# One transfer for x of batch 1, ahead of the clearing of the padded state tile

## The chip, the cores and the metric

The kernel runs on one core of a Trainium2 chip. Its time is the device time of one execution in microseconds (us); shorter is better. The core has TensorE (PE, with its weight loads listed as PEld), VectorE (DVE), ScalarE (ACT), GpSimd (POOL) and SyncE (SP). Each takes its own instructions in order and waits for the others by semaphores. SP, ACT and GpSimd also issue DMA transfers, each into a queue of its own: in the profile q1 is SP's, q10 ScalarE's and q0 GpSimd's. All three queues are served by the same 16 DMA engines.

## The reference

```python
# x (8, 8, 512, 64), state (8, 8, 32, 64): batches, heads, rows, width
scores = scale * x @ state^T;  a  = softmax(scores);   xread = a @ state
scores2 = scale * state @ x^T; a2 = softmax(scores2);  sread = a2 @ x
attn = concat([xread, sread], rows)            # 512 + 32 rows a batch
x = attn.transpose(0, 2, 1, 3).reshape(4352, 512)
out = (1 / (1 + exp(-(x @ w_gate))) * (x @ w_val)) @ w_out   # 512 -> 1536 -> 512
```

Each batch is a small attention of its rows against 32 state rows for each of eight heads, and of the state rows against the batch's rows; all 4352 rows then pass through one gated layer. Results are float32.

## The kernel before

The whole program is unrolled, and every engine's instructions stand in the order in which the function calls them: a hand-written sequence of small helpers, most with the batch as first argument. Batches 0 and 1 are worked on together in the opening, batches 2 to 7 and the state rows (as a ninth round) follow in a regular loop of twelve steps each. The gated layer never multiplies the attention output by the weights directly: `sw_visit` and its relatives multiply the state by the gate and value weights (tile `SW`), and `gv_mm` multiplies these by the transposed attention weights `aT`, so that the output of the two comes from one product.

The opening does this for batch 0:

- `load_xp(0, nc.sync, lo, n)` (L87) loads x of batch 0 in four transfers of two heads each on SP, in the order heads 0-1, 4-5, 2-3, 6-7. `load_s(0, nc.scalar)` (L524) loads the state of batches 0 and 1 on ScalarE's queue.
- `cast_xp` (L95) casts each quarter to bf16: heads 0-1 and 6-7 on ScalarE, 4-5 and 2-3 on VectorE. `xT_mm` (L132) transposes it on TensorE with the identity `ident`, and `xT_cp` (L135) copies the result out.
- `Sq_mm` (L174) gives the scores of two heads, `Sq_exp` (L182, ScalarE) their exponentials, `nq_sum` (L186 and L188, VectorE) the sums and reciprocals, `nq_mul` (L193, VectorE or GpSimd) the product. On ScalarE all four `Sq_exp` of batch 0 are called behind the cast of heads 6-7.
- `aT_mm` (L234) transposes the attention weights, `aT_cp` (L244) copies them out, and `gv_mm` (L343) and `sw_visit` (L293) can run.

x of batch 1 does not come through SP. `load_xh` (L100) loads it on GpSimd's queue, which turns float32 into bf16 on the way, into the tile `xh` (named `xf` in the profile). `xT_mm(1, 0, ...)` transposes heads 0-3 of it, `xT_mm(1, 2, ...)` heads 4-7. On TensorE the order there is: transposes of heads 6-7 of batch 0, `xT_mm(1, 0)`, the last scores of batch 0, three warm-up matmuls, `xT_mm(1, 2)`.

GpSimd's queue also carries the weights, in the order in which they are needed: `load_w` (L104) eight times with 256 columns and twice with 512, and `load_sb` (L527) with the state of later batches, then x of batch 2 and the output weights. Behind them lie the first casts and products that GpSimd computes itself.

`zero(sbz, pool)` (L111) clears the tile `sbz`, a part of `tw`, in which the state of batches 2 to 7 stands between zeros; `load_sb` writes into it later. `make_identity` writes `ident`. `warm` (L517) issues matmuls on a cleared tile; the first eight stand at the start of TensorE's order.

Of the kernel before, what the change touches and what calls it, by code (L numbers as in the profile page):

```python
# [16 lines left out]
def kernel(  # L17
# [45 lines left out]
    sbz = tw[:, :27 * D].rearrange("p (q d) -> p q d", q=3)  # L63
# [11 lines left out]
    vec, act, pool = nc.vector.tensor_copy, nc.scalar.copy, nc.gpsimd.tensor_copy  # L75
# [13 lines left out]
    def xh_tile(b):  # L89
        if b not in xhs:  # L90
            xhs[b] = stg.tile((128, H, 4, D), BF, name="xf", padded_shape=(128, 2 * H, 4, D))

    def cast_xp(b, cp, lo, n):
        xh_tile(b)
        cp(xhs[b][:, lo:lo + n], xfs[b][:, lo:lo + n])  # L95

    def load_xh(b, lo, n):
        xh_tile(b)
        v = x[b].rearrange("h (p c) d -> p h c d", c=4)
        nc.gpsimd.dma_start(xhs[b][:, lo:lo + n], v[:, lo:lo + n])  # L100
# [9 lines left out]
    def zero(t, eng):  # L110
        (nc.gpsimd if eng is pool else nc.vector).memset(t, 0.0)  # L111
# [401 lines left out]
    def warm(n, place):  # L513

        ps = place[0].tile((128, 512), FP, name="warm", tag=place[1])
        for _ in range(n):
            nc.tensor.matmul(ps.rearrange("p (r k) -> p r k", r=4), wm, wm.unsqueeze(1).to_broadcast((128, 4, 128)), start=True, stop=True)  # L517
# [46 lines left out]
    load_s(0, nc.scalar)  # L564
    nc.vector.memset(wm, 0.0)
    warm(4, S1)
    zero(sbz, pool)
    warm(4, S1)
    make_identity(nc, ident)
    load_xh(1, 0, 4)  # L570
    nc.vector.memset(ones, 1.0)
    cast_s(0, vec)
    cast_xp(0, act, 0, 2)
    load_xh(1, 4, 4)
    zero(sTd, vec)
    sT_mm(0, S1)
    load_xp(0, nc.sync, 4, 2)
# [459 lines left out]
```

## Time and profile before

| | |
|---|---|
| median of 3 runs | 213.55 us |
| lowest, highest | 213.36, 213.91 us |
| span of the profiled execution, first to last instruction | 212.3 us |
| what lies around the span, by the median | 1.25 us |
| TensorE busy in the span | 204.3 us (96%) |
| VectorE, ScalarE, GpSimd busy | 160.3, 129.6, 78.1 us |
| DMA | 27.14 MB, 128 GB/s over the span |

The profile records one execution; of its own time it gives the span alone. Times in its rows are counted from the span's start. A row of the timeline gives start, length, engine, line, operation, the output and the input tile, and in brackets how long the engine had stood idle and what ended that. The chain of waits follows the work that ended last back to what released it at each step. The view of the DMA queues counts packets in a window of time; 1024 packets of 1 KB are x of batch 0.

### The profile page before, as it was taken

The numbers are of one execution on the slowest core, as the hardware profiler recorded it, in microseconds if no ns is written. First come the engines' busy times: TensorE is split into PE (matmuls) and PEld (weight loads), VectorE is DVE, ScalarE is ACT, GpSimd is POOL, SyncE is SP. The second block draws the span as 40 slices with busy tenths as digits, with TensorE's granted clock in tenths as the row PEclk, the third lists the DMA queues.
The fourth block names the chain that finished last, engine by engine and source line by source line (L and its number), as shares of the span: only waits on it lengthen the run. The fifth ranks groups of instructions, "written<-read, shape, count | busy, mean of one in ns | idle before, by whom it ended". The sixth has DMA issues, their size and how long they took to land.

```text
span 212.3 us, 5333 instructions
## 1 busy us (share of the span) xinstructions
PE 204.3 (96%) x2089; PEld 132.9 (63%) x2089; DVE 160.3 (76%) x308; ACT 129.6 (61%) x244; POOL 78.1 (37%) x103
## 2 busy tenths in 40 slices
PE   7779999999999999999999999999999999999991
PEld 2545443677666666575666566657566666788981
DVE  2598899998987788578866887688748876865681
ACT  3878898754767477856786578647764663333210
POOL 8799458599042705900491029201500000000000
PEclk9999999999999999999999999999999999999998
DMA  6999999662589943996822621273110400221133
GB/s 205 163 192 191 214 289 183 119 212 40 78 224 333 136 91 110 302 94 208 249 42 48 173 99 28 58 120 153 29 31 35 166 2 0 99 102 49 39 112 99
DMA packets 41320, 27.14 MB, mean 128 GB/s; under 512 B 23632, under 2 KB 39248, under 8 KB 41296
## 3 DMA queue, kind: packets, MB, share of 16 engines
q1 hardware_dynamic: 31088, 20.00, 36.9%
q0 software_dynamic: 9776, 6.49, 19.8%
q10 hardware_dynamic: 432, 0.33, 0.6%
q8 instruction: 16, 0.26, 0.5%
q14 instruction: 8, 0.07, 0.1%
HBM read 18.35 MB, written 8.91 MB: 128 GB/s over the span
## 4 chain that ended last, share of the span: by engine, by line
PE 91%; DMA 3%; DVE 2%; ACT 1%; SPq 1%; issue 0%
PE gvp L355 30%; PE outp L425 29%; PE gvp L343 10%; PE gvp L358 5%; PE outp L442 4%; PE swp L286 4%; DMA xf<-in_x_dram 3%; PE swp L293 2%; PE outp L484 2%; PE Sp L147 1%; PE outp L467 1%; PE rdp L262 1%; SPq L87 1%; DVE rsq L186 1%; PE aTp L234 1%; PE rdp L265 1%
## 5 line engine op out<-in xcount | busy, mean ns | idle before, releaser
L369 DVE SCALAR_TENSOR_TENSOR glu<-th,gvp 128x512 bf16<-128x512 f32 (+1 forms) x108 | 70.1, 655 | 36.7 <-PE gvp L355 13.7
L364 ACT ACTIVATE th<-gvp 128x512 f32<-128x512 f32 (+1 forms) x108 | 62.1, 578 | 49.3 <-PE gvp L355 34.8
L355 PE MATMUL gvp<-aT,SW 128*128 128x512 bf16 x288 | 77.4, 379 | 0.1
L329 ACT CAST SW<-swp 128x512 bf16<-128x512 f32 x83 | 46.5, 592 | 9.3 <-PE swp L286 8.3
L425 PEld LDWEIGHTS <-Sm 128*128 128x128 bf16 x324 | 31.7, 98 | 12.6
L355 PEld LDWEIGHTS <-SW 128*128 128x128 bf16 x288 | 26.7, 98 | 17.3 <-issue 3.6
L200 POOL CAST Eb<-E 128x256 bf16<-128x256 f32 x32 | 12.8, 438 | 52.0 <-ACT E L167 52.0
L425 PE MATMUL outp<-tw,Sm 128*128 128x256 bf16 x240 | 31.8, 273 | 0.0
L425 PEld LDWEIGHTS <-glu 128*128 128x128 bf16 x240 | 23.5, 98 | 10.2
L425 PE MATMUL outp<-wo,glu 128*128 128x256 bf16 x168 | 22.9, 273 | 0.0
L343 PE MATMUL gvp<-aT,SW 128*128 128x512 bf16 x96 | 22.6, 379 | 0.0
L227 POOL TENSOR_TENSOR ab<-E,ri 128x512 bf16<-128x512 f32 x13 | 14.3, 1100 | 11.8 <-DVE ri L210 7.1
L407 DVE TENSOR_TENSOR Sm<-glu 128x768 bf16<-128x768 bf16 (+1 forms) x34 | 18.0, 535 | 0.0
L433 DVE SCALAR_TENSOR_TENSOR res<-outp,U 128x512 f32<-128x512 f32 x22 | 15.0, 685 | 1.2 <-PE outp L442 0.9
L343 PEld LDWEIGHTS <-SW 128*128 128x128 bf16 x96 | 8.6, 97 | 10.4 <-issue 1.8
L116 POOL CAST xb<-xf 128x1024 bf16<-128x1024 f32 x12 | 13.2, 1128 | 1.9 <-DMA xf<-in_x_dram 1.9
L358 PE MATMUL gvp<-xb,wgv 128*128 128x256 bf16 x96 | 12.6, 272 | 0.0
L167 ACT ACTIVATE E<-Sp 128x512 f32<-128x512 f32 x14 | 8.4, 599 | 6.7 <-PE Sp L147 5.7
L425 PE MATMUL outp<-wo,Sm 128*128 128x256 bf16 x84 | 11.5, 273 | 0.0
L358 PEld LDWEIGHTS <-wgv 128*128 128x128 bf16 x96 | 9.3, 98 | 1.3
L251 POOL CAST xs<-xf 128x1024 bf16<-128x1024 f32 x10 | 10.2, 1044 | 0.0
L425 PE MATMUL outp<-tw,glu 128*128 128x256 bf16 x72 | 9.8, 273 | 0.0
(105 smaller groups left out, 213.3 us busy)
## 6 DMA issues: line engine op xcount, KB each, us to landing
out_dram<-res SPq DMA_DIRECT2D x14, 512.0 KB, 3.4
xf<-in_x_dram SPq DMA_DIRECT2D x5, 1024.0 KB, 7.5
wo<-in_moe_w_out_dram POOLq DMA_DIRECT2D x3, 512.0 KB, 7.8
xf<-in_x_dram SPq DMA_DIRECT2D x4, 256.0 KB, 3.9
wgv<-in_moe_w_gate_dram POOLq DMA_DIRECT2D x4, 256.0 KB, 7.7
wgv<-in_moe_w_val_dram POOLq DMA_DIRECT2D x4, 256.0 KB, 8.8
xf<-in_x_dram POOLq DMA_DIRECT2D x1, 1024.0 KB, 9.5
out_dram<-res SPq DMA_DIRECT2D x3, 256.0 KB, 2.2
```

The costliest lines, as they stand in the source:

```text
L116: cp(xbs[b].rearrange("p c h d -> p h c d")[:, lo:lo + n], (xhs if b in xhs else xfs)[b][:, lo:lo + n])
L200: nc.gpsimd.tensor_copy(Ebs[b][:, c], E1s[b][:, c])
L227: (nc.gpsimd if eng is pool else nc.vector).tensor_tensor(half(b, i, abs_), e1, ri.unsqueeze(len(ri.shape)).to_broadcast(e1.shape), ALU.mult)
L329: cp(*sw_left.pop((b, lo, w, e)))
L343: nc.tensor.matmul(ps, SWs[b][:, g, w, fs], aTs[b][:, :, g], start=(g == 0), stop=(g == 1))
L355: nc.tensor.matmul(ps, SWs[b][:, g, w, fs], aTs[b][:, :, g], start=(g == 0), stop=(g == 1))
L358: nc.tensor.matmul(ps, (wg, wv)[w][:, j, fs], held["XS"][:, j], start=(j == 0), stop=(j == 3))
L364: nc.scalar.activation(th, held["gv", b, f][0], AF.Tanh, scale=0.5)
L369: nc.vector.scalar_tensor_tensor(glus[b][:, f], held["th", b, f], 1.0, held["gv", b, f][1], ALU.add, ALU.mult)
L407: eng.tensor_tensor(S_(b, t)[:, i], a, c, op)
L425: nc.tensor.matmul(wps[key][:, c], lhs[:, i, c * 128:(c + 1) * 128], rhs[:, i], start=(first and c == 0 and i == 0), stop=(i == NF // 2 - ...
L433: nc.vector.scalar_tensor_tensor(to, wps[key], 0.5, held["w", name], ALU.mult, ALU.add)
```

## The change

GpSimd's first work is put in another order, and x of batch 1 is loaded by one transfer of eight heads instead of two of four.

```diff
     load_s(0, nc.scalar)
     nc.vector.memset(wm, 0.0)
     warm(4, S1)
-    zero(sbz, pool)
     warm(4, S1)
     make_identity(nc, ident)
-    load_xh(1, 0, 4)
+    load_xh(1, 0, 8)
+    zero(sbz, pool)
     nc.vector.memset(ones, 1.0)
     cast_s(0, vec)
     cast_xp(0, act, 0, 2)
-    load_xh(1, 4, 4)
     zero(sTd, vec)
     sT_mm(0, S1)
```

On GpSimd, the opening of its order after the program's own constants; `tw` is the tile cleared, `xf` here x of batch 1 and `wgv` the gate and value weights:

```order
-L111 MEMSET tw 128x1728
 masks.py:197 MEMSET ident 128x128
 masks.py:199 ISA
 masks.py:199 AFFINE_SELECT ident<-ident 128x128
-L100 DMA xf<-in_x_dram 128x4x256 x2
+L100 DMA xf<-in_x_dram 128x8x256
+L111 MEMSET tw 128x1728
 L104 DMA wgv<-in_moe_w_gate_dram 128x4x256
 L104 DMA wgv<-in_moe_w_val_dram 128x4x256
```

The clearing moves from the head of the queue to behind the one transfer of x, and ahead of all weights; the identity and the transfer move up by one place.

On TensorE, the second group of transposes of x of batch 1 (`xT_mm(1, 2)`), behind the three warm-up matmuls; `DMASW1` is the semaphore of GpSimd's second transfer:

```order
 L517 LDWEIGHTS wm
 L517 MATMUL warm<-wm 128x512
-L132 LDWEIGHTS xf [waits DMASW1_49]
+L132 LDWEIGHTS xf
 L132 MATMUL xTp<-ident,xf 128x128 [waits PE_49]
 L132 LDWEIGHTS xf
```

The wait for the second transfer is gone there. The first group (`xT_mm(1, 0)`) waits for GpSimd's first transfer as before, which is now the whole of x of batch 1. The order of the instructions on TensorE, VectorE, ScalarE and SP is unchanged.

## The prediction

> **What bounds the kernel now.** I read the page first, then the busy time by stretch, then the chain of waits over the opening, then the order of the opening on GpSimd, then the packets of the DMA queues in short windows.
>
> From the page and from the view of busy time by stretch (stretch, its length, then each engine's busy us):
>
> ```profile
> span 212.3 us, 5333 instructions
> ...
> 14.00:207.00 193.00, 192.87 (x1977) 126.50 (x1977) 151.71 (x284) 120.88 (x229) 65.81 (x81) 1.00 0.55 124
> ```
>
> From 14 us to 207 us TensorE is busy 192.87 of 193 us. So nothing that starts earlier or later behind 14 us is worth much; what counts is when TensorE reaches that dense stretch. The chain of waits (start, length, what) tells what sets this moment:
>
> ```profile
> 2.27 5.45 DMA xf<-in_x_dram
> 7.72 0.02 issue
> 7.74 0.62 ACT xf L95
> ...
> 10.97 1.06 DVE ab L193 x2
> 12.03 0.14 issue
> 12.17 0.62 PE aTp L234 x8
> ...
> 17.16 3.45 PE gvp L343 x16
> ```
>
> The chain hangs on the fourth and last quarter of x of batch 0 (call the quarters P1 to P4 in the order of their issue on SP; P4 is heads 6 and 7). P4 is issued at 2.27 and lands at 7.72. ScalarE stands waiting for it with all exponentials of batch 0 queued behind the cast; then VectorE runs the four sums and reciprocals and two products without a break to 12.03, and TensorE's transposes of the attention weights begin at 12.17. If P4 lands later by some amount, every step to 14 us moves by that amount, and the dense stretch with it.
>
> **The change, part by part.** On GpSimd, in order of time (start, length, engine; the wait before it in brackets):
>
> ```profile
> 0.73 1.54 POOL L111 MEMSET tw<- 128x1728 bf16 x1 [0.29 <-POOLq L1021]
> 2.21 0.20 POOL masks.py:197 MEMSET ident<- 128x128 bf16 x1
> 2.49 0.29 POOL masks.py:199 TENSOR_SCALAR_AFFINE_SELECT ident<-ident 128x128 bf16<-128x128 bf16 x1
> 2.73 1.68 POOL L100 DMA_DIRECT2D xf<-in_x_dram  x2
> 4.39 0.75 POOL L104 DMA_DIRECT2D wgv<-in_moe_w_gate_dram  x1
> ...
> 21.92 0.93 POOL L82 DMA_DIRECT2D xf<-in_x_dram  x1
> ```
>
> GpSimd is free at 0.73. The identity takes 2.21 to 2.73 now, 0.52; so x of batch 1 is issued at 0.73 + 0.52 = 1.25 in place of 2.73, 1.48 earlier. Two issues cost 1.68; one of the same eight-head shape, later in the trace, costs 0.93, so the clearing starts at 2.18 and ends at 3.72. The first weight issue then stands at 3.72, 0.67 before today's 4.39.
>
> ```profile
> 0.99 3.81 PE L517 MATMUL warm<-wm 128*128 128x512 bf16 x8 [0.99 <-DVE ones L571]
> ```
>
> The identity earlier: worth nothing, its first user (the transposes of the state) waits for these eight warm-up matmuls, to 4.80.
>
> ```profile
> 3.61 0.29 DVE L532 CAST sb<-sf 128x256 bf16<-128x256 f32 x1 [2.66 <-DMA sf<-in_state_dram]
> ```
>
> The clearing later: at most 0.1 on this cast of the state, which may have to wait until 3.72 if the two engines hold each other up, hidden by the same matmuls; were that cover gone it would cost its 0.1. The state load that now waits for the clearing is the fifth issue behind it, at about 6.8, long after 3.72.
>
> The price is in the DMA engines. The view of the DMA queues (q1 is SP's, q0 GpSimd's; packets, MB, share of 16 engines) from 0 to 5.19 us, all its rows:
>
> ```profile
> q1 hardware_dynamic: 943, 0.92, 51.6%
> q10 hardware_dynamic: 144, 0.13, 9.9%
> ```
>
> from 5.19 to 5.5, q0's row:
>
> ```profile
> q0 software_dynamic: 32, 0.02, 38.5%
> ```
>
> from 3 to 5, q1's row:
>
> ```profile
> q1 hardware_dynamic: 756, 0.73, 107.0%
> ```
>
> from 6.3 to 7.45, all:
>
> ```profile
> q0 software_dynamic: 262, 0.13, 86.0%
> q1 hardware_dynamic: 12, 0.01, 3.6%
> ```
>
> and from 3.72 to 8, q1's row:
>
> ```profile
> q1 hardware_dynamic: 693, 0.66, 46.7%
> ```
>
> (q10 is ScalarE's queue with the state.) Before 5.19 q0 moves nothing: its first packet comes 5.19 - 2.73 = 2.46 after the issue. By the same 2.46 it comes at 1.25 + 2.46 = 3.71 in the changed kernel. From 3 to 5 us q1 alone fills all 16 engines: 756 packets in 16 x 2 us, 42 ns a packet on one engine. So x of batch 1 finds no free engine when it comes earlier; it takes turns with P2 to P4. What a turn costs is seen from 6.3 to 7.45: q1 has 12 packets left, 3.6% of 16 engines, which is 58% of one engine: the last quarter on one late engine, every packet behind one of q0's: 1.15 us / 12 = 96 ns instead of 42.
>
> ScalarE's cast of P1, which starts when P1 is there:
>
> ```profile
> 4.16 0.62 ACT L95 CAST xf<-xf 128x512 bf16<-128x512 f32 x1 [1.67 <-DMA xf<-in_x_dram]
> ```
>
> When P4 lands then, by two readings of these rows. An engine of the mean: 693 packets of q1 are left at 3.72, 43 for each engine, at 96 ns 4.15 us, so 7.87, and with the 0.27 from the last packet's window (7.45) to the landing (7.72) it is 8.15: 0.43 late. The late engine: P1 is used at 4.16, and the 48 packets of P2 to P4 that each engine has then (1024 packets in all, 64 to an engine, 16 to a quarter) take 48 x 0.096 = 4.6: 8.77, or 8.97 if P1's last four packets pay their turns too. A landing needs all 16 engines, so I go by the late one and take 8.85: **1.13 late**. The bound below is 0.0 (q1 not disturbed); the one above is the late engine sharing all its 64 packets from its start, 4.16 less 0.29 for the tail and 16 x 0.042 = 3.2: 3.2 + 6.14 + 0.29 = 9.63, 1.91 late.
>
> P2 and P3 come late as well (by 0.9 and 1.4 on the same count), but their transposes and scores only fill time in which ScalarE waits for P4; they are not on the path while P4 is the last.
>
> One landing for x of batch 1. Its use now, from the weight loads of TensorE:
>
> ```profile
> 8.81 0.45 PEld L132 LDWEIGHTS <-xf 128*128 128x128 bf16 x8 [0.17 <-DMA xf<-in_x_dram]
> ...
> 10.37 0.45 PEld L132 LDWEIGHTS <-xf 128*128 128x128 bf16 x8 [0.43 <-DMA xf<-in_x_dram]
> ```
>
> TensorE's first eight transposes of it (8.81) used to need the first half and now need all of it, and the last scores of batch 0 stand behind them in TensorE's order. The late engine is through with q1 at 8.85 - 0.29 = 8.56 and has served (8.56 - 3.71) / 0.096 = 50 of its 64 packets of batch 1; 14 more at 42 ns end at 9.15, landing about 9.45. TensorE gets there at 8.81 + 1.13 = 9.94. So it costs nothing, 0.5 of cover; if that is gone and it lands as late as the second half does now (used at 10.37), it costs 10.37 - 9.94 = 0.43. The second eight (10.37) lose their wait, and gain nothing: VectorE copies them out only at the end of its products.
>
> What is gained: the weights behind x of batch 1 come up to 0.9 earlier (9.45 against its use at 10.37 now). The dense stretch has one place where TensorE waits for them:
>
> ```profile
> 20.69 1.89 PE L343 MATMUL gvp<-aT,SW 128*128 128x512 bf16 x8
> 22.60 0.62 PE L293 MATMUL swp<-wgv,tw 64*32 64x512 bf16 x16
> ```
>
> Eight matmuls from 20.69 end at 22.58, the next starts at 22.60 where the pace of such matmuls (17.16 in the chain above: 16 in 3.45, 0.216 each) would give 20.69 + 8 x 0.216 = 22.42. **0.18 back.** With the stretch itself 1 us later this wait is surely gone.
>
> Sum on the profiled execution: 212.3 + 1.13 - 0.18 = 213.25 of span. The runs' median lies 213.55 - 212.3 = 1.25 above this span, which I take as what lies around it: **214.5 us**, 0.95 or 0.44% slower.
>
> **The rivals.** *No late engine.* The lag of one engine may be an accident of this execution. Then the mean engine decides: +0.43 - 0.18 = +0.25, 213.8. For it: 15 engines had finished before 6.3. Against: a landing takes the last of 16, and some engine is always last.
>
> *The SP quarters are not disturbed* (the other side: not slower). If q0 waits while q1 has packets, P4 loses even the turns that it pays today. It would land near 7.72 - 12 x 0.054 = 7.07 or earlier, and ScalarE's own wait is the limit of the gain:
>
> ```profile
> 7.74 0.62 ACT L95 CAST xf<-xf 128x512 bf16<-128x512 f32 x1 [0.34 <-DMA xf<-in_x_dram]
> ```
>
> The chain gains 0.34 at most; with the 0.18 the time is 213.03, and under 212.9 if the weights' lead removes some more small gaps. It decides from the point where q1's pace stays at 42 ns while q0 moves. Against it stand the 12 packets at 96 ns. The Trainium skill, page "DMA: Bandwidth & Descriptors", section on queues, rings and completion order, also says that each engine goes round robin over the queues that have work, packet by packet.
>
> *x of batch 1 starts sooner still.* Its issue runs from 2.73 to 4.41 now, beside VectorE's cast at 3.61; at 1.25 to 2.18 VectorE has nothing to do but wait for the state (2.66 of wait before 3.61). If the 2.46 us hold a wait for VectorE, the late engine shares from its start: the upper bound, +1.91 - 0.18, 215.3. The Trainium skill, page "SBUF — State Buffer", section on the two separate sides, has such a rule: descriptors for GpSimd's queue are not written while VectorE holds the shared port. No row before shows which part of the 2.46 that would be, so I give it little.
>
> *TensorE's rate falls.* With 1.1 us more of waiting TensorE does little from 5.2 to 9.9:
>
> ```profile
> 7.00:8.00 1.00, 0.52 (x12) 0.41 (x12) 0.31 (x1) 0.66 (x2) 1.00 (x2) 1.00 0.82 108
> ```
>
> and at 9.62, among TensorE's matmuls:
>
> ```profile
> 9.62 0.81 PE L517 MATMUL warm<-wm 128*128 128x512 bf16 x3
> ```
>
> At the start eight matmuls take 3.81 (0.48 each), at 9.62 three take 0.81 (0.27 each). If the slow rate came back, the first 3.81 us of work would cost 3.81 x (1 - 0.27 / 0.48) = 1.7 more: 214.5 + 1.7 = 216.2. For it: the busy share would sink under the 0.52 of the emptiest us today. Against: at 0.52 nothing slowed down. The Trainium skill, page "TensorE: Matmul & The Clock Gate", part 1, lets the rate halve after an idle window of about 3.4 us; no stretch here would be idle that long, so I give it least.
>
> **How the numbers follow.** Chances: the forecast 0.52 (its own range 214.1 to 215.0), no late engine 0.15, SP undisturbed 0.20, sooner still 0.07, slow TensorE 0.06. A measurement here tells 0.3%, 0.64 us, from no change: faster is below 212.9, slower above 214.2. Faster: 0.13 of the undisturbed case's 0.20, since 213.03 lies close to the bound and the weights' lead is not fully counted. Slower: 0.48 of the forecast, 0.01 of the second case, 0.13 of the last two: 0.62. The rest, 0.25, is no change. The range runs from 213.0, which holds half of the undisturbed case, to 215.3, which holds half of the sooner one: 0.10 below it and 0.09 above it are left out.
>
> **What would show it.** Right: q0's first packet near 3.7; q1 at about half its pace from there; P4 used by ScalarE near 8.85; the products, the transposes of the weights and the dense stretch each about 1.1 later; no wait at the weight matmuls now at 22.60. Wrong: ScalarE's cast of P4 still near 7.7 (then no contention), or its landing late and the dense stretch not, which would mean slack that I didn't see; or x of batch 1 landing after 9.9 and becoming the last wait itself; or matmuls near 0.48 again after 9 us.

## The result and the profile after

| | before | after |
|---|---|---|
| median of 4 runs each, same chip | 213.73 us | 217.31 us |
| lowest, highest | 213.36, 214.42 us | 216.13, 217.79 us |
| ratio, 95% interval | | 1.0140 (1.0098 to 1.0182) |
| span of the profiled execution | 212.3 us | 215.4 us |
| P4, the last quarter of x of batch 0: issue, landing | 2.27, 7.72 | 2.27, 10.77 |
| transposes of the attention weights begin | 12.17 | 15.40 |

The change makes the kernel 1.4% slower by this ratio; the two medians lie 3.58 us, 1.7%, apart. 214.5 us was forecast, and at most 215.3: the sign was right, the size much too small.

The chain of waits over the opening, after (start, length, what); the prediction shows the same view of the kernel before:

```profile
2.27 8.50 DMA xf<-in_x_dram
10.77 0.02 issue
10.80 0.63 ACT xf L95
...
11.47 0.62 PE xTp L132 x4
...
14.30 0.97 DVE ab L193 x2
15.27 0.14 issue
15.40 0.62 PE aTp L234 x8
...
20.40 3.45 PE gvp L343 x16
```

It is the same chain through the same transfer. P4 is issued at 2.27 as before, but takes 8.50 us to its landing, not 5.45: 3.05 later. The transposes of the attention weights are 3.23 later, the 16 products that stood at 17.16 are 3.24 later, the span 3.1 longer. Nearly all that is lost is lost in one transfer, and the dense stretch hands it on whole:

```profile
17.00:210.00 193.00, 192.72 (x1976) 126.31 (x1976) 151.66 (x284) 121.10 (x230) 66.03 (x81) 1.00 0.54 122
```

TensorE is busy 192.72 of 193 us there, as it was 192.87 of 193 from 14 us on.

GpSimd's opening and the casts, after, from the timeline (start, length, engine; in brackets the idle time before and what ended it):

```profile
0.73 0.20 POOL masks.py:197 MEMSET ident<- 128x128 bf16 x1 [0.29 <-POOLq L1020]
1.01 0.29 POOL masks.py:199 TENSOR_SCALAR_AFFINE_SELECT ident<-ident 128x128 bf16<-128x128 bf16 x1
1.44 1.08 POOL L100 DMA_DIRECT2D xf<-in_x_dram  x1
2.51 1.56 POOL L111 MEMSET tw<- 128x1728 bf16 x1
3.57 0.65 DVE L532 CAST sb<-sf 128x256 bf16<-128x256 f32 x1 [2.62 <-DMA sf<-in_state_dram]
...
10.80 0.62 ACT L95 CAST xf<-xf 128x512 bf16<-128x512 f32 x1 [3.98 <-DMA xf<-in_x_dram]
11.47 1.46 PE L132 MATMUL xTp<-ident,xf 128*128 128x128 bf16 x12 [2.56 <-ACT xf L95]
```

The change did what it says: x of batch 1 (x1 below) is issued at 1.44 in place of 2.73. ScalarE's wait for P4 grew from 0.34 to 3.98 us. TensorE's twelve transposes from 11.47, four of P4 and eight of x1, run without a break; x1 landed at 11.07, just before they ask for it.

The packets by queue (q1 is SP's with x of batch 0, q0 GpSimd's with x1 and the weights), from 4.2 to 5.3 us. Before:

```profile
q1 hardware_dynamic: 400, 0.39, 105.3%
q0 software_dynamic: 8, 0.00, 2.7%
```

After:

```profile
q1 hardware_dynamic: 227, 0.21, 57.0%
q0 software_dynamic: 122, 0.06, 55.7%
```

Until 4.2 both kernels had moved nearly as much of q1 (576 packets and 567 of 1088: the 1024 of x, and 64 small ones that go with its transfers). Then q0's first packet comes, at 4.30 after and at 5.20 before, and q1 falls back. After, from 5.0 to 6.25 us:

```profile
q0 software_dynamic: 316, 0.16, 107.9%
q1 hardware_dynamic: 29, 0.03, 8.2%
```

Here the forecast's picture breaks. With turns packet by packet, q1 should have about as many packets as q0 while both have work. It has 29 against 316, and 271 more of q1, most of them P4's, come only after 6.25. For more than a microsecond P4 is hardly served. From 0 to 6 us, q1's row before, then after:

```profile
q1 hardware_dynamic: 1062, 1.03, 50.5%
q1 hardware_dynamic: 811, 0.78, 39.7%
```

At 6 us, 277 of q1's 1088 packets are still to come after the change; P4 with its small packets makes up 272. Where P4 is served, however, its packets pay what was forecast. After, from 9.8 to 10.5 us, q1's row:

```profile
q1 hardware_dynamic: 8, 0.01, 3.9%
```

3.9% of 16 engines is 62% of one: again one late engine. In the trace these eight packets start 95 ns apart; the forecast had 96. Seventeen starts at this distance lead from 8.96 to 10.49, which reads as this engine's whole share of P4 (16 packets and a small one). So P4 is late because engines take it up late, the last of them near 9 us, and not because a turn is dearer than forecast.

### The profile page after: what moved, and what is told of

Read it like the earlier page. It is cut to its first block, busy times and chain, and to the rows that moved or that the text cites. A ratio compares the mean times of both kernels' runs of the same rounds, so it can differ in the third digit from the quotient of the medians.

```text
span 215.4 us, 5332 instructions
## 1 busy us (share of the span) xinstructions
PE 204.6 (95%) x2089; PEld 133.6 (62%) x2089; DVE 160.7 (75%) x308; ACT 129.6 (60%) x244; POOL 77.6 (36%) x102
## 4 chain that ended last, share of the span: by engine, by line
PE 90%; DMA 4%; DVE 1%; ACT 1%; SPq 1%; issue 0%
PE gvp L355 29%; PE outp L425 28%; PE gvp L343 10%; PE gvp L358 5%; PE outp L442 4%; DMA xf<-in_x_dram 4%; PE swp L286 4%; PE swp L293 2%; PE outp L484 2%; PE Sp L147 1%; PE outp L467 1%; PE rdp L262 1%; SPq L87 1%; PE aTp L234 1%; PE rdp L265 1%; ACT aT L244 1%
## 5 line engine op out<-in xcount | busy, mean ns | idle before, releaser
L200 POOL CAST Eb<-E 128x256 bf16<-128x256 f32 x32 | 12.8, 437 | 52.1 <-ACT E L167 52.1
L343 PEld LDWEIGHTS <-SW 128*128 128x128 bf16 x96 | 8.7, 98 | 10.5 <-issue 1.9
```

The source lines that it names most:

```text
L200: nc.gpsimd.tensor_copy(Ebs[b][:, c], E1s[b][:, c])
L343: nc.tensor.matmul(ps, SWs[b][:, g, w, fs], aTs[b][:, :, g], start=(g == 0), stop=(g == 1))
```

## The experiments

Throughout, x0 is x of batch 0, and "quarters" are its four transfers. Edits are against the changed kernel where nothing else is said. No kernel leaves work out; three add warm-up matmuls. Each ratio is to the kernel before on the same chip (213.55 to 213.71 us). Two things were changed at once, the place of x1's issue and the number of its transfers, and the first four runs take them apart.

**One part alone: the early issue, in two transfers.**

```diff
     make_identity(nc, ident)
-    load_xh(1, 0, 8)
+    load_xh(1, 0, 4)
+    load_xh(1, 4, 4)
     zero(sbz, pool)
```

> The changed order, but x of batch 1 again as two transfers of four heads, both ahead of the clearing. Theory A (the early start of GpSimd's queue holds off the quarters of x of batch 0 that SP has not moved by then): still slow, P4 used by ScalarE after 10 us, 216.3 to 217.8 us. Theory B (the one long transfer does it, since it leaves SP's queue no gap): back to the time before, P4 used by 8.9, 213.4 to 214.5 us.

Measured: 216.04 us (215.69 to 217.7, four runs), ratio 1.0128 (1.0088 to 1.0168). q0's first packet came at 4.54, and the chain starts with P4 again:

```profile
2.27 7.47 DMA xf<-in_x_dram
9.76 0.63 ACT xf L95
```

P4 lands at 9.74, 2.0 late. P3 is late too: it lands at 8.18, in the kernel before at 5.94 (after the change at 6.82). The early issue is enough for most of the loss.

**The other part alone: one transfer, behind the clearing** (edit of the kernel before):

```diff
-    load_xh(1, 0, 4)
+    load_xh(1, 0, 8)
...
-    load_xh(1, 4, 4)
```

> The order before (clearing first), with x of batch 1 as one transfer of eight heads in the place of the first of the two. Theory A (early start): as before, P4 used by 8.2 us, 213.4 to 214.4 us. Theory B (one long transfer): slow, P4 used after 9.5 us, 216 to 217.8 us.

Measured: 216.16 us (215.31 to 217.34, four runs), ratio 1.0122 (1.0076 to 1.0168). This part by itself costs nearly as much, which I had not expected. P4 is early here (6.42; q0's first packet at 5.48), and the chain runs another way:

```profile
2.73 6.57 DMA xf<-in_x_dram
9.35 1.03 PE xTp L132 x8
...
11.74 1.71 DVE ab L193 x2
...
13.58 0.62 PE aTp L234 x8
```

The transfer on the chain is now x1, issued at 2.73 and landed at 9.30. TensorE's first eight transposes of x1 stand in its order ahead of the last scores of batch 0, and all that follows waits with them: 9.35 in place of 8.81, although only half of the data is used there. Then the eight take 1.03 us (eight take 0.62 at 10.37 in the kernel before; here the granted clock is half from 9.28 to 12.69), and VectorE's two products take 1.71 instead of 1.06. Casts of GpSimd's own (L200, 11.52 to 13.16) run beside them; that they are the cause was not tried by itself. The transposes of the attention weights are 1.41 later.

**Half of the clearing ahead of the one transfer,** so that the issue lies between the two places:

```diff
+    zero(tw[:, :864], pool)
     make_identity(nc, ident)
     load_xh(1, 0, 8)
-    zero(sbz, pool)
+    zero(tw[:, 864:27 * D], pool)
```

> The changed order with half of the clearing moved back to the head: GpSimd's queue starts about 0.8 us later than in the changed kernel and 0.1 to 0.2 before the place that it had before the change. Theory A with a start time from which it decides: P4 used at 8 to 9 us and 214 to 215 us, since most of P4 is then under way. Theory B: still one long transfer, P4 used after 9.5 us and over 216 us.

Measured: 215.91 us (215.39 to 216.75, four runs), ratio 1.0104 (1.0069 to 1.0138). The issue is at 2.01, q0's first packet at 5.22, P4 lands at 7.57 as in the kernel before, and the chain goes through x1 with 8.76 us from issue to landing. So an issue 0.7 us earlier than before brings q0's first packet no earlier and does P4 no harm; the next 0.6 us, to 1.44, bring it to 4.30 and do the harm. A late P4 goes with an early first packet of q0, and not with the time since the issue; whether q0's packets hold P4's back, or fill a place that P4's leave empty, these runs don't tell.

**P4 through ScalarE's queue,** behind the state:

```diff
     load_s(0, nc.scalar)
+    load_xp(0, nc.scalar, 6, 2)
...
-    load_xp(0, nc.sync, 6, 2)
```

> The changed kernel with P4 (heads 6 and 7 of batch 0) issued on ScalarE's queue behind the state, not as SP's fourth. If P4 was late because SP's queue handed it out late (queue theory): P4 is used by 7.5 us, P3 becomes the last quarter, 213.4 to 214.5 us. If P4 was late because every packet of it pays turns to GpSimd's queue (turn theory, as in the prediction): it is used at 8.5 to 10.8 whatever queue it is in, 214.5 to 217.3 us.

Measured: 216.59 us (215.84 to 216.99, four runs), ratio 1.0134 (1.011 to 1.0158). P4 lands at 5.12, now early, but the transfer that is last on SP takes its place:

```profile
1.76 7.15 DMA xf<-in_x_dram
8.94 0.44 DVE xf L95
```

It lands at 8.92; from 6 us on only 26 packets of SP's queue are left, and 19 of them come after 7.5. q0's first packet came at 5.37 here, so its time alone does not tell whether a transfer will be late. In this run the last transfer on SP is late, and P4 on another queue is not. I take it that those packets of SP's queue are late which the engines do not yet have when q0's come; no run shows this.

**TensorE kept at its full rate** by 17 more warm-up matmuls in its waits (seven behind the transposes of heads 4-5, ten behind the last scores before the transposes of P4):

```diff
     xT_mm(0, 2, OU)
+    warm(7, G0)
...
     Sq_mm(0, 1, AT)
+    warm(10, G0)
```

> The changed kernel with 17 warm-up matmuls on TensorE in the two stretches in which it waits there for P3 and P4 (7 behind the transposes of heads 4 and 5, 10 behind the scores of heads 2 and 3), so that it stays busy. Theory A (P4's landing sets the time, the half clock costs only what it adds between the landing and the dense stretch, 0.2 us in the two profiles): clock 1.00 through 7 to 14 us, P4 as late as in the changed kernel, 216.2 to 217.3 us. Theory C (the half clock is the main loss): at least 1.5 us faster than the changed kernel, 214 to 215.7 us.

Measured: 217.27 us (216.96 to 218.63, four runs), ratio 1.0152 (1.0113 to 1.0191). The granted clock stayed at 1.0, but the ten matmuls came too late themselves:

```profile
10.97 2.16 PE warm L517 x10
13.13 0.24 PE xTp L132 x4
```

They held P4's transposes up to 13.13. As a price of the rate this tells nothing. It does show that P4 is late (11.08, q0's first packet 4.21) with TensorE at full rate too, and P3 with it (9.26).

**The same with 11 matmuls** (seven and four):

```diff
+    warm(7, G0)
...
-    warm(10, G0)
+    warm(4, G0)
```

> The changed kernel with 11 warm-up matmuls in TensorE's two waits (7 and 4, so that they end before the data they fill the time for). Theory A (P4's landing sets the time): full rate through the opening, 216.5 to 217.5 us. Theory C (the half rate is the main loss): under 215.7 us.

Measured: 216.95 us (215.99 to 218.34, four runs), ratio 1.0156 (1.012 to 1.0192). The fillers are off the path now, and the chain is that of the changed kernel at full rate:

```profile
2.27 8.04 DMA xf<-in_x_dram
10.34 0.62 ACT xf L95
...
14.75 0.62 PE aTp L234 x8
```

From P4's landing (10.31) to the transposes of the attention weights it takes 4.44 us, in the kernel before 4.45 (7.72 to 12.17), in the changed kernel 4.63 (10.77 to 15.40). The half rate therefore costs the changed kernel about 0.2 on its path, and the rest of the loss is there without it.

**x0 in two transfers on SP,** heads 0-3 and 4-7, instead of four:

```diff
-    load_xp(0, nc.sync, 0, 2)
+    load_xp(0, nc.sync, 0, 4)
+    load_xp(0, nc.sync, 4, 4)
...
-    load_xp(0, nc.sync, 4, 2)
...
-    load_xp(0, nc.sync, 2, 2)
...
-    load_xp(0, nc.sync, 6, 2)
```

> The changed kernel with x of batch 0 as two transfers of four heads on SP in place of four of two. Hand-out theory (once GpSimd's queue runs, SP's next transfer is handed to the engines late, so a transfer that is handed out before that is safe): heads 4 to 7 are handed out by 1.7 us, land by 7.5, and what is left over the time before is x of batch 1 in one landing: 214 to 216 us. Turn theory (each packet pays turns): heads 4 to 7 still land at 8.5 to 9.5 us, 215 to 217 us.

Measured: 216.16 us (215.07 to 216.37, four runs), ratio 1.0095 (1.0058 to 1.0131). x1 is issued at 1.44 as in the changed kernel, yet from 4.2 to 5.3 us the view of the queues has one row of the two:

```profile
q1 hardware_dynamic: 384, 0.39, 108.2%
```

q0 moves nothing; its first packet comes at 5.38, and heads 4-7 land at 6.04, undisturbed. So an early issue does not by itself bring q0's packets early. That SP's queue without a break keeps them off is my reading, not shown. The lateness of P4 is cured, and what is left is x1:

```profile
1.44 8.28 DMA xf<-in_x_dram
9.76 1.03 PE xTp L132 x8
```

The chain starts with x1 as in the second run, with the eight transposes at half the rate (1.03). It goes on through batch 1's own scores (L156, at 13.14) and their exponentials, as in the run with the last scores moved, below.

**The same with x1 in two transfers,** both early:

```diff
-    load_xh(1, 0, 8)
+    load_xh(1, 0, 4)
+    load_xh(1, 4, 4)
```

> The order of the changed kernel with x of batch 0 in two transfers of four heads and x of batch 1 in two as well, both early. If the single landing of x of batch 1 is what keeps the kernel with x of batch 0 in two slow (215.1 to 216.4): its first half now lands at 7.5 to 8.3 us, the transposes of it are no wait, 213.0 to 214.0 us. If the early start is still at work: above 215 us.

Measured: 214.24 us (213.94 to 214.47, twelve runs), ratio 1.0026 (1.0017 to 1.0036). x1 lands in halves at 8.09 and 9.41, and the chain runs through x0 and VectorE as in the kernel before:

```profile
1.26 5.20 DMA xf<-in_x_dram
...
11.28 1.06 DVE ab L193 x2
12.47 0.62 PE aTp L234 x8
```

With x0 in two transfers and x1 in halves the early issue is nearly free.

**The kernel before with x0 in two transfers,** the fair partner of the last run (the edit of x0 above, made on the kernel before):

> The kernel before with x of batch 0 as two transfers of four heads on SP (x of batch 1 in its two transfers, behind the clearing). Both theories of P4 let it land by about 6.5 us; ScalarE then waits no more for it, which is worth at most the 0.34 us of its wait before: 213.1 to 213.6 us. Slower than 214.2 would say that the other quarters, which now land as halves, are on the path.

Measured: 214.13 us (213.74 to 214.42, twelve runs), ratio 1.0011 (0.9996 to 1.0025). Same as before, and above what was expected: the last landing comes at 6.40 instead of 7.72, but heads 4 and 5 land with it, which VectorE used from 4.91 on in the kernel before, and the chain goes through them. The transposes of the attention weights begin at 12.28. Beside this run, the early issue in the run above costs about 0.1 us, which the two intervals do not tell from nothing.

These runs fill a square:

| x0 | x1 | issue behind the clearing | issue ahead of it |
|---|---|---|---|
| quarters | two transfers | 1 (the kernel before) | 1.0128 |
| quarters | one transfer | 1.0122 | 1.0140 (the change) |
| halves | two transfers | 1.0011 | 1.0026 |
| halves | one transfer | not run | 1.0095 |

There are two causes, either of which costs some 2.5 us, and both together 3.6: the later of two landings, P4's or x1's, sets the end, so they don't add up. The intervals of the three ratios overlap; that both together cost more than one is not shown.

**The last scores of batch 0 ahead of x1's transposes,** with the one late transfer of the second run:

```diff
     xT_mm(0, 3, S3)
-    xT_mm(1, 0, S0, 2)
...
     Sq_mm(0, 3, OU)
+    xT_mm(1, 0, S0, 2)
```

> The kernel with one transfer in the old place (clearing first), and on TensorE the last scores of batch 0 (heads 6 and 7) ahead of the first transposes of x of batch 1, so that they don't wait for the single landing. If that landing is what made the one transfer in the old place slow (its profile: landing at 9.30, the scores behind it): 213.0 to 214.0 us, and it may pass the kernel before, since P4 landed at 6.42 there. If something else did (the clock, the weights): still 215 to 217 us.

Measured: 215.6 us (214.07 to 216.94, eight runs), ratio 1.0085 (1.0048 to 1.0122). This is lower than the second run, but the intervals overlap, and x1 landed later in this profile (10.27 against 9.30), so the worth of the exchange stays open. The expected return to 213.0 to 214.0 did not come. Batch 0's last scores no longer wait for x1, and the chain is still x1's:

```profile
2.73 7.54 DMA xf<-in_x_dram
10.31 1.03 PE xTp L132 x8
...
13.48 0.44 PE Sp L156 x8
```

Behind x1's transposes stand batch 1's own scores (L156) and their exponentials, which ScalarE has in its order ahead of the copies that batch 0's products need. TensorE's order is one of two places that wait for x1; ScalarE's is the other.

**The same exchange in the kernel before:**

> The kernel before with the same exchange on TensorE alone (two transfers). There the scores did not wait for the first half of x of batch 1 (0.13 us of slack on VectorE), so all theories expect no change: 213.2 to 213.9 us. It says how much of the run above is the exchange itself.

Measured: 214.1 us (213.3 to 214.59, twelve runs), ratio 1.0007 (0.9988 to 1.0026). No change: with x1 in halves, nothing in the kernel before waits at this place that another wait would not take over.

**x0 in two transfers, with six warm-up matmuls ahead of x1's transposes,** to find the half rate's share in that kernel:

```diff
     xT_mm(0, 3, S3)
+    warm(6, G0)
     xT_mm(1, 0, S0, 2)
```

> The changed order with x of batch 0 in two transfers, and 6 warm-up matmuls on TensorE while it waits for x of batch 1. There the chain from that landing on ran on TensorE at half rate (8 transposes 1.03, three warm-up matmuls 1.47). If the half rate is what that costs: full rate again, 1.0 to 1.4 us less, 214.6 to 215.3 us. If the landing alone does it: 215.6 to 216.5 us.

Measured: 216.65 us (215.95 to 217.19, four runs), ratio 1.0145 (1.0121 to 1.017). A miss: x1 landed at 9.87, but the fillers ran mostly at half rate themselves (the granted clock is half to 11.09) and held its transposes up:

```profile
9.60 2.09 PE warm L517 x6
11.69 0.45 PE xTp L132 x8
```

What half the rate costs where x1 is the last wait stays open.

## Why the prediction was right or wrong

**What bounds the kernel: right.** P4's landing, the chain to the transposes of the attention weights and a dense stretch that passes every delay on: each of the three stands in the profile after, by 3.05, 3.23 and 3.24 us.

**When q0 starts: wrong, in two ways.** The issue came at 1.44, not 1.25: from the identity's first instruction to the issue it takes 0.71, where I carried 0.52 over from the kernel before; there the issue's row starts 0.05 ahead of the end of the second instruction, here 0.14 behind it. More important, I carried the 2.46 us from issue to first packet over as if it belonged to GpSimd's queue. From these five kernels it is anything between 2.5 and 3.9:

| kernel | issue of x1 | first q0 packet | last of x0 lands |
|---|---|---|---|
| after | 1.44 | 4.30 | 10.77 |
| x1 in two, early | 1.44 | 4.54 | 9.74 |
| half of the clearing | 2.01 | 5.22 | 7.57 |
| before | 2.73 | 5.20 | 7.72 |
| x0 in two, x1 one, early | 1.44 | 5.38 | 6.04 |

Over all fourteen kernels the first packet comes between 5.15 and 5.48, with the issue anywhere from 1.44 to 2.73, but for four kernels: those with the issue at 1.44 and four quarters on SP, where it comes between 4.21 and 4.64.

**What a shared engine costs P4: the step that failed.** The term was +1.13: the late engine was to take the 48 packets of P2 to P4 from 4.16 on without a break, each at 96 ns instead of 42. It measured +3.05, beyond the bound of 1.91 that I gave it. The price of a turn held: 95 ns between P4's last packets. What failed is the run without a break. P2 landed at 4.85, as before (4.89) and not 0.9 late; P3 landed 0.88 late; then q1 got 29 packets against 316 in 1.25 us. At 95 ns an engine's 16 packets of P4 take 1.5 us, so the last engine, if it ran through, began P4 only near 9.0 (an estimate from the end of its packets at 10.5), where I had it done with all of q1 at 8.56. The twelve packets of the kernel before, from which the price came, told nothing of this wait. The Trainium skill, page "DMA: Bandwidth & Descriptors", section on queues, rings and completion order, says that each engine goes round over the queue rows that have work, packet by packet (a packet there holds several descriptors; the view's are single pieces of 1 KB or less). The 95 ns agree with turns, piece by piece; the 29 against 316 do not contradict them if P4's packets were not yet there to be chosen, which is what halves instead of quarters suggest (all of x0 landed by 6.04 with the same early issue). What keeps them back, no run shows, and it stays open. The bound above assumed that a turn is the worst that a competitor can do, and that is why the range was too short.

**The one landing: right in the changed kernel, by accident.** I gave it no cost because P4 would be later still. So it was: x1 landed at 11.07, TensorE came at 11.47. But the cover is all P4's lateness. With P4 on time the one landing costs 1.2% (second run), where I had 0.43 us for a cover that is gone. I compared the landing with the time at which TensorE gets there, and counted neither the half rate that the wait brings nor ScalarE's order, in which batch 1's exponentials come ahead of batch 0's copies.

**TensorE's rate: the rival came true, at another price.** The stretches of 1 us after (length, then busy time of TensorE, its weight loads, VectorE, ScalarE and GpSimd; then the granted clock):

```profile
4.00:5.00 1.00, 0.85 (x12) 0.36 (x11) 0.83 (x3) 0.62 (x1) 1.00 (x3) 1.00 1.12 310
5.00:6.00 1.00, 0.72 (x8) 0.38 (x8) 0.30 (x1) 0.96 (x2) 1.00 (x2) 1.00 1.15 148
6.00:7.00 1.00, 0.00 (x0) 0.00 (x0) 0.16 (x1) 0.79 (x2) 1.00 (x2) 1.00 1.21 167
7.00:8.00 1.00, 0.61 (x8) 0.61 (x9) 0.66 (x2) 0.00 (x0) 1.00 (x3) 0.67 1.18 213
8.00:9.00 1.00, 0.82 (x12) 0.50 (x9) 0.42 (x1) 0.00 (x0) 0.56 (x1) 0.50 1.27 209
```

The clock falls to half at 7.34 and stays there to 14.17. I gave this 6 chances in 100 and priced it at 1.7. It happened, and it cost 0.2, by the run with 11 fillers. The chain says why: from P4's landing to the transposes of the attention weights only four transposes on it are TensorE's, 0.62 us; all else there is VectorE's and ScalarE's. I had priced the rate as if TensorE's first 3.8 us of work all lay on the path.

**The clearing beside VectorE's cast** cost more than the 0.1 I allowed (0.65 us in place of 0.29), and was hidden behind the eight warm-up matmuls, as said.

**The wait at the weight matmuls** is gone as forecast, but gave back 0.09, not 0.18. Before, the eight products from 20.69 were 1.91 ahead of the weight matmuls; after, the rows that answer these are

```profile
23.92 1.89 PE L343 MATMUL gvp<-aT,SW 128*128 128x512 bf16 x8
...
25.74 0.14 PEld L293 LDWEIGHTS <-tw 64*32 64x32 bf16 x16 [0.42 <-issue]
25.74 0.63 PE L293 MATMUL swp<-wgv,tw 64*32 64x512 bf16 x16
```

1.82 apart. Half of the 0.18 was pace, not wait.

**What lies around the span: mis-sized.** In the profiled execution after, 217.23 - 215.4 = 1.83, and it was 1.74 to 1.84 in each profiled execution of the experiments. I had 1.25, because I set the span of one execution against the median of others; by 1.8 that execution took 214.1, the upper part of what this kernel shows (213.36 to 214.42).

The terms add up: 212.3 + 3.05 (P4) + 0.18 (the half rate) - 0.09 (the weights) = 215.4, the span measured; with 1.83 around it 217.2, the time of that execution. Of the 2.8 us by which the forecast was short, P4 makes 1.9, the part around the span 0.6, the rate 0.2 and the weights 0.1.

**The other rivals fell.** "Not disturbed" would have P4 no later than 7.72. "Sooner still" would have q0 start before 3.71; it started at 4.30, and P4 was nevertheless later than that rival's bound. A wait for VectorE does not explain the different starts of q0: in the changed kernel and in the one with x0 in two transfers VectorE's cast of the state ends at 4.22 and its own clearing runs from 4.27 and 4.28 to 4.76, yet the first packet comes at 4.30 in the one and at 5.38 in the other. No version that was run beats the kernel before; the two closest (1.0007 and 1.0011) cannot be told from it.

## What to carry to other kernels

When a transfer is issued earlier on another queue, ask not only what a turn costs the transfers of the critical queue, but also when the engines will take up those that are still to come. Here the turns cost what was forecast, and a transfer of 256 KB was still 3 us late; two transfers of 512 KB in place of four of 256 KB were not held up. Joining two landings into one costs whatever the engine that uses the first half has behind it in its order, and there can be two such engines. A price per packet, times the packets, is the time of an engine that never waits: give the sum a bound that does not rest on that.

## What the runs showed of the hardware

- The engines did not serve the two queues alike: 29 packets of SP's queue against 316 of GpSimd's in 1.25 us, while a 256 KB transfer of the former, issued at 2.27, was still mostly to come. Once it was served, its packets on the last engine started 95 ns apart, as in the kernel before beside GpSimd's queue (96), against 42 with SP's queue alone.
- The time from issue to first packet on GpSimd's queue is no constant: 2.47 us in the kernel before and 2.54 with x0 in two transfers (issue 2.73 in both), 2.86 after and 3.94 with x0 in two transfers (issue 1.44 in both). What sets it stays open.
- TensorE's clock halved although TensorE had been busy for about half of the time: by the stretches above some 1.6 us of the 3.4 us before 7.34, with no wait longer than 1.7 us. It then stayed at half for 6.83 us, twice 3.41. The Trainium skill, page "TensorE: Matmul & The Clock Gate", part 1, asks for an idle window of about 3.4 us; the length of the steps agrees with these rows, the idleness does not.
- The granted clock can miss such a stretch: with x0 in two transfers its column shows 1.00 throughout, while eight 128x128 transposes take 1.03 us instead of 0.62 and three warm-up matmuls 1.47 instead of 0.81. The trace has no clock record there before 13.71. The lengths of equal matmuls are the surer sign.
- VectorE's cast of the state took 0.65 us beside GpSimd's clearing, in other kernels with the early issue 0.60 to 1.44, and 0.29 to 0.42 where the clearing was over. Beside the clearing it ended 0.14 to 0.15 us behind it each time, however early it had begun (3.14 to 3.61). The Trainium skill, page "SBUF — State Buffer", section on the two separate sides, has the pair of ports that these two engines share as a lock for whole instructions, and these rows agree.
